# Attention with beacons and a gelu MLP on one core: first loads moved to the hardware DMA queue, and the first MLP group one pair of heads earlier

## The chip, the cores and the metric

The kernel runs on one core of a Trainium2 chip. The metric is device time in microseconds (us), and lower is better. The engines are TensorE (PE; its weight loads are shown as PEld), VectorE (DVE), ScalarE (ACT), GpSimd (POOL) and SyncE (SP). Transfers that POOL issues run on the software DMA queue, those that SP and ACT issue on the hardware queue.

## The reference

There are 8 batches, 8 heads, 576 queries, 16 beacon keys and head width 64. All inputs are float32.

```python
scale = 1.0 / np.sqrt(D)
k_all = np.concatenate([beacon_k, k], axis=2)          # 16 + 576 keys
v_all = np.concatenate([beacon_v, v], axis=2)
scores = scale * np.matmul(q, k_all.transpose(0, 1, 3, 2))
causal = np.zeros((S, Nb + S), dtype=bool)
causal[:, Nb:] = np.triu(np.ones((S, S), dtype=bool), k=1)
scores = np.where(causal, -1000000000.0, scores)
a = np.exp(scores - scores.max(-1, keepdims=True))
a /= a.sum(-1, keepdims=True) + 1e-09
attn_out = np.matmul(a, v_all)
x = attn_out.transpose(0, 2, 1, 3).reshape(B * S, H * D)   # 4608 x 512
h = x @ w_in                                               # w_in 512 x 2048
g = h * (1.0 / (1.0 + np.exp(-1.702 * h)))
out = g @ w_out                                            # w_out 2048 x 512
```

## The kernel before

**Tiles and steps.** Attention is worked in 32 steps, one for each pair of heads: pair i belongs to batch i // 4. In one step, `qk_chunk` (L289) makes the transposed scores in four chunks into the two PSUM buffers `s`; `exp_chunk` (L302, ACT) turns them into `E` in float16; `mask_chunk` cuts the causal diagonal out, on DVE (L318, a minimum with the tile `keep`) or on POOL (L325). `av_half` (L359) multiplies by V in four parts (two heads, two halves of the queries) into the PSUM ring `u`, which has four banks. The V tile `vb` carries 64 columns of ones beside each head's values, so the row sums of the exponentials come out of the same matmul; `ones` (L101) writes these columns once. `av_out` (L370) copies the four parts to an `O` buffer (three of them). Then DVE normalises: `z_turn` (L382, tile `zt`, twice), `z_recip` (L388, `rt`), `z_back` (L392, `rz`) and `norm` (L401, twice) write the result into `xT`.

The MLP takes 512 tokens as a group, nine groups in all. `mlp1` (L428) makes 16 tiles of the hidden layer, `mlp1_gelu` (L440, ACT) writes them to `g`, `mlp2` (L450) makes four output tiles of 16 matmuls each, which are copied to `osb` (L461, L463) and stored by SP (L468). Exponential and gelu need different ACT tables, so each change between them costs an `ACT_TABLE_LOAD`. Matmul results of the MLP use the same four `u` banks as AV.

**How q, k and V come in.** All inputs are cast to float16 on the way in, by the software queue that POOL issues. Batches 0 and 1 (`NB2` = 2) are loaded by `load_qk6` (L130) into a buffer `g`, six tokens to a partition row; PE transposes them (`tr_pe`, L148) and `tr_pe_out` (L156) copies them to `qT` and `kT`. Batch 0 is loaded as heads 0 to 2, 2 to 4 and 4 to 8, batch 1 at once. Their beacon keys come by `load_bk6` (L136, tile `bkn`), are transposed by PE (L165) and copied by DVE (L168). From batch 2 on, `load_qk` (L114, tiles `n0` for q and `n1` for k) loads four heads at a time; DVE transposes 32 x 32 squares (L211, `sq`), DVE or POOL puts them in order (L220, `t0`, `t1`), SP writes them to DRAM (L230, `d`) and reads them back in place (L237). The beacon keys of these batches come by `load_bk` (L120) into `bk`, which has 32 rows for each head of four, 16 of them zero, and DVE transposes them (L226). V comes by `load_v` (L176 for beacons, L179 in five pieces), the weights by `load_w1` (L186) and `load_w2` (L193) in four pieces each.

**The order.** Each engine runs its instructions in order. That order is written at build time by a planner: every piece of work is a `Work` with an engine (or a choice of engines), an assumed duration, a key (when it is due), the works it `needs` and those it comes `after`, and a buffer that it takes. `issue` (from L792) repeatedly takes the work that can start first by the planner's own clock. The list `ends` says behind which pair each MLP group comes: with `ends[0] = 6`, group 0 follows the scores of pair 5; its four output tiles are placed in the four pairs ahead of the next group, pairs 7 to 10. Group 1 follows the scores of pair 10. `FILL` matmuls on a tile of zeros (`warm`, L865) may be put where the planner sees PE idle in the first 60 us; 42 are placed. The program keeps eight semaphores for the software queue's transfers, so each transfer that POOL issues first waits until the eighth before it has landed, and whatever stands behind it on POOL waits as well.

Of the kernel before, what the change touches and what calls it, by code (L numbers as in the profile page):

```python
# [9 lines left out]
F16 = mybir.dt.float16  # L10
F32 = mybir.dt.float32
AFT = mybir.ActivationFunctionType
ALU = mybir.AluOpType
# [3 lines left out]
def kernel(  # L17
# [11 lines left out]
    nc = tc.nc  # L29
# [28 lines left out]
    VMASK = 8  # L58
# [41 lines left out]
    def ones(t):  # L100
        nc.vector.memset(t[:, :, :, D : 2 * D], 1.0)  # L101
# [16 lines left out]

    def load_bk(x):
        nc.gpsimd.dma_start(  # L120
            out=bks[x * SQ + Nb : (x + 1) * SQ, NB2:B, :, :].rearrange("n b g d -> n (b g) d"),
            in_=beacon_k[NB2:B].rearrange("b (g x) n d -> x n (b g) d", x=HG)[x],
        )
# [11 lines left out]
    def load_bk6():  # L135
        nc.gpsimd.dma_start(  # L136
            out=bkn.rearrange("n b h d -> n (b h) d"),
            in_=beacon_k[0:NB2].rearrange("b h n d -> n (b h) d"),
        )
# [21 lines left out]
    def tr_pe_beacon(b):  # L161
        u = psu.tile([P, NPAIR, Nb], F16, tag="u", name="u")
        tru[b] = u
        for p in range(NPAIR):
            nc.tensor.transpose(u[:, p, :], bkn[:, b, 2 * p : 2 * p + 2, :], ident[0:Nb, 0:Nb])  # L165

    def tr_pe_beacon_out(b):
        nc.vector.tensor_copy(out=kTs[b % 2][:, :, 0:Nb], in_=tru[b][:, :, :])  # L168
# [197 lines left out]

    def av_out(i, x, half, eng):
        if i not in Os:
            Os[i] = op_.tile([P, 2, S], F32, tag="O", name="O")
        copy[eng](  # L370
            out=Os[i][:, x, AQ[half] : AQ[half + 1]], in_=avu[(i, x, half)][:, :]
        )

# [121 lines left out]
    SPL, CAP = 2.5, 2.0  # L495

    def use(buf, *ws):
        buf.users += ws
# [6 lines left out]
    pk = {}  # L505
    mkeep = Work("POOL", 0.3, -4.95, make_keep)
    midn = Work("POOL", 0.6, -5.95, lambda: make_identity(nc, ident))

    bk6 = Work("POOL", 0.57, -5.97, load_bk6, dma=0.25)

    def first_loads(b):
        k0 = 4 * b
        kl = (-6, -4.4)[b]
        gb6 = Buf("g")
        lds = {}
        for (h0, h1) in ((0, 2), (2, 4), (4, H)) if b == 0 else ((0, H),):
            for w in (1, 0):
                x = Work(
                    "POOL", 0.7, kl + 0.1 * h0 + 0.02 * (1 - w) + (h0 == 4),
                    lambda b=b, h0=h0, h1=h1, w=w: load_qk6(b, h0, h1, w),  # L520
                    alloc=gb6 if not lds else None, dma=0.37 * (h1 - h0),
                    after=list(lds.values())[:1],
                )
                for p in range(h0 // 2, h1 // 2):
                    lds[(p, w)] = x
        ub = Buf("u")
        x = Work("PE", 0.3, k0, lambda b=b: tr_pe_beacon(b), [bk6, midn], alloc=ub)
        y = Work("DVE", 0.25, k0, lambda b=b: tr_pe_beacon_out(b), [x], alloc=kTb[b])
        use(ub, y)
        for p in range(NPAIR):  # L530
            for w in (1, 0):
                ub = Buf("u")
                kk = 4 * b + p - 0.5
                x = Work(
                    "PE", 0.55, kk, lambda b=b, p=p, w=w: tr_pe(b, p, w), [lds[(p, w)], midn],
                    alloc=ub, after=[x],
                )
                use(gb6, x)
                z = Work(
                    dict(ACT=0.66, DVE=0.76), 0, kk,  # L540
                    lambda eng, b=b, p=p, w=w: tr_pe_out(b, p, w, eng),
                    [x], alloc=qTb[b] if (w, p) == (0, 0) else None,
                    after=[y] if w == 1 else [pk[(b, 0, 0)]] if p else (),
                )
                use(ub, z)
                pk[(b, p, w)] = z
        pk[b] = y

    for b in range(B):
# [5 lines left out]
        for g in range(2) if b >= NB2 else ():  # L555
            for w in (1, 0):
# [25 lines left out]
                if w == 1:  # L582
                    if bkB is None:
                        bkB = [
                            Work("POOL", 0.55, 4.3, lambda x=x: load_bk(x), after=[ld_], dma=0.2)
                            for x in range(HG)
                        ]
                    need = [Work(
                        "DVE", 0.25, k0, lambda b=b, g=g: tr_beacon(b, g),
                        bkB, after=cp[:1],  # L590
                    )]
# [35 lines left out]
    on = [Work("DVE", 2.7, (0.2, 1.5)[x], lambda x=x: ones(vbs[x])) for x in range(2)]  # L627
# [9 lines left out]
    for i in range(NSTEP):  # L637
# [36 lines left out]
        Ob, zb = Buf("O"), [Buf("zt"), Buf("rt"), Buf("rz")]  # L674
        evs = []
        zn = []
        for x in range(2):
            for half in range(2):
                mm = av_list(x, half)
                u_ = Buf("u")  # L680
                js = sorted({j for (j, lo, hi, col) in mm})
                av = Work(
                    "PE", sum(hi - lo for (j, lo, hi, col) in mm) / 2400 + 0.05,
                    i + 1.05 + 0.2 * x + 0.1 * half,
                    lambda i=i, x=x, half=half: av_half(i, x, half),
                    [r for j in js for r in ready[j]] + vb_, alloc=u_, after=avs[-1:],
                )
                avs.append(av)
                avp.setdefault(i, []).append(av)
                use(Eb, av)  # L690
                use(vbb[b], av)
                evs.append(Work(
                    dict(DVE=0.45, ACT=0.46), 0, i + 0.5,
                    lambda eng, i=i, x=x, half=half: av_out(i, x, half, eng), [av],
                    alloc=Ob if not evs else None, after=evs[:1],
                ))
                use(u_, evs[-1])
            zn.append(Work(
                "DVE", 0.74, i + 0.48, lambda i=i, x=x: z_turn(i, x), evs[-2:],
                alloc=zb[0] if not zn else None, after=zn[:1],  # L700
            ))
        zr = Work("DVE", 0.2, i + 0.45, lambda i=i: z_recip(i), zn, alloc=zb[1])
        zk = Work("DVE", 0.75, i + 0.45, lambda i=i: z_back(i), [zr], alloc=zb[2])
        use(Ob, *zn)
        use(zb[0], zr)
        use(zb[1], zk)
        for x in range(2):
            nw = Work(
                dict(DVE=0.78), 0, i + 0.45, lambda eng, i=i, x=x: norm(i, x, eng),
                [zk], alloc=xTb[b] if p + x == 0 else None,  # L710
                after=[norms[b * NPAIR][0]] if p + x else (),
            )
            norms.setdefault(i, []).append(nw)
            use(zb[2], nw)
            use(Ob, nw)
# [3 lines left out]

    ends = [6, 11, 15, 19, 23, 27, 31, 32, 32]
# [69 lines left out]
    def issue():  # L792
        free = dict(PE=1.0, ACT=1.0, DVE=1.0, POOL=0.7, SP=0.7)
        landed = dict(POOL=[0.0] * 8, SP=[0.0] * 8)
        given = {r: [] for r in rings}
        dma_free = dict(POOL=0.0, SP=0.0)
# [3 lines left out]
        while todo:  # L800
# [43 lines left out]
            if w.dma:  # L844
                f = max(dma_free[eng], t + d + dict(SP=0.7, POOL=1.6)[eng]) + w.dma
                dma_free[eng] = f
                w.t1 = f + dict(SP=SPL, POOL=0.4 if t < 40 else 1.0)[eng]
                landed[eng].append(w.t1)
# [12 lines left out]
    nc.vector.memset(bks, 0.0)  # L861
# [38 lines left out]
```

## Time and profile before

| what | value |
|---|---|
| median of 13 runs | 378.74 us (376.81 to 379.7) |
| profiled execution | 379.7 us, span 378.0 us |
| busy PE, DVE, ACT, POOL | 359.5, 256.0, 232.4, 153.4 us |
| software queue | 18.62 MB, 47.4% of 16 engines over the span |
| hardware queue | 23.79 MB, 19.3% |
| first exponential | starts at 9.56 us |
| first matmul of MLP group 0 | 43.09 us |
| first output matmul (L450) | 63.80 us |
| MLP group 1 begins | about 94.6 us |

The span is what the profile covers; the execution's own time is 1.7 us longer. The page divides the span into 40 slices of 9.45 us; a digit is the busy share of a slice in tenths. "The chain of waits" follows the work that ended last back in time. A group such as `128x576 f16<-128x576 f16` gives the shapes of what is written and read. Times to landing are from the issue on the engine to the end of the transfer. MB of the software queue are counted in float16, as written.

### The profile page before, as it was taken

The page shows a single profiled execution, that of the slowest core. Times are in us where ns is not written, and L with a number is a line of the kernel's source. Part 1 is how long each engine was busy: PE and PEld are TensorE (multiplying, and loading weights), DVE is VectorE, ACT ScalarE, POOL GpSimd, SP SyncE. Part 2 cuts the span into 40 slices and gives each one's busy share as a digit, 9 for nine tenths or more (in the row PEclk, how much of TensorE's full clock was granted, in tenths as well). Part 3 has the DMA queues.
Part 4 walks back from the last instruction along what each step waited for, and adds up shares of the span by engine and source line. Part 5 has one row for each costly group of instructions (what it writes and reads, how often), then busy time and mean ns, then how long its engine had stood idle before and what let it go on. Part 6 is the DMA issues. An engine that isn't in the chain of part 4 may idle for free.

```text
span 378.0 us, 6003 instructions
## 1 busy us (share of the span) xinstructions
PE 359.5 (95%) x2290; PEld 177.4 (47%) x2290; DVE 256.0 (68%) x421; ACT 232.4 (61%) x345; POOL 153.4 (41%) x271
## 2 busy tenths in 40 slices
PE   7896999859999999999999999999999999999995
PEld 3443544325444444444444784444454454444442
DVE  5479896398998996899779976992698075000021
ACT  3878868425877587658765776677676743626300
POOL 9866763456256923592368235820331010000000
PEclk9967799989999999999999999999999999999999
DMA  8999799939459974596559855962010002000012
GB/s 88 165 205 167 104 208 242 219 69 138 98 161 246 139 166 141 116 128 127 180 109 134 147 155 117 128 113 62 30 56 29 0 29 83 0 29 28 27 58 83
DMA packets 68908, 42.79 MB, mean 113 GB/s; under 512 B 41744, under 2 KB 61200, under 8 KB 68880
## 3 DMA queue, kind: packets, MB, share of 16 engines
q0 software_dynamic: 50640, 18.62, 47.4%
q1 hardware_dynamic: 18240, 23.79, 19.3%
q8 instruction: 18, 0.29, 0.3%
q14 instruction: 10, 0.08, 0.1%
HBM read 44.40 MB, written 16.61 MB: 161 GB/s over the span
## 4 chain that ended last, share of the span: by engine, by line
PE 71%; DVE 12%; DMA 10%; POOL 4%; ACT 2%; issue 1%; POOLq 0%
PE u L428 29%; PE u L450 28%; PE u L359 8%; PE s L289 5%; DMA w<-in_moe_w_out_dram 4%; DMA n<-in_k_dram 3%; DVE zt L382 3%; DMA g<-in_k_dram 3%; DVE xT L401 2%; ACT E L302 2%; DVE O L370 2%; POOL vb L179 1%; DVE t L220 1%; DVE rz L392 1%; DVE sq L211 1%
## 5 line engine op out<-in xcount | busy, mean ns | idle before, releaser
L302 ACT ACTIVATE E<-s 128x1024 f16<-128x1024 f32 (+3 forms) x128 | 104.1, 864 | 48.6 <-PE s L289 47.3
L450 PE MATMUL u<-w,g 128*128 128x512 f16 x576 | 130.0, 380 | 0.2 <-DMA w<-in_moe_w_out_dram 0.2
L428 PE MATMUL u<-xT,w 128*128 128x512 f16 (+1 forms) x640 | 126.5, 358 | 0.0
L440 ACT ACTIVATE g<-u 128x512 f16<-128x512 f32 x144 | 85.3, 597 | 43.3 <-PE u L428 42.9
L325 POOL TENSOR_SCALAR_AFFINE_SELECT E<-E 128x256 f16<-128x256 f16 (+2 forms) x153 | 63.7, 435 | 87.7 <-ACT E L302 87.6
L428 PEld LDWEIGHTS <-w 128*128 128x128 f16 x640 | 61.9, 98 | 60.6 <-issue 0.9
L450 PEld LDWEIGHTS <-g 128*128 128x128 f16 x576 | 54.5, 98 | 65.8 <-issue 4.7
L463 DVE COPY osb<-u 128x512 f32<-128x512 f32 x29 | 19.8, 682 | 66.6 <-PE u L450 66.4
L359 PE MATMUL u<-E,vb 128*128 128x336 f16 (+4 forms) x448 | 57.7, 275 | 7.2 <-DVE osb L463 3.6
L370 DVE COPY O<-u 128x240 f32<-128x240 f32 (+1 forms) x88 | 36.8, 439 | 33.2 <-PE u L359 30.5
L359 PEld LDWEIGHTS <-vb 128*128 128x128 f16 (+1 forms) x448 | 38.3, 100 | 30.0 <-issue 15.1
L382 DVE STREAM_TRANSPOSE zt<-O 64x576 f32<-64x576 f32 x64 | 49.3, 770 | 3.1 <-ACT O L370 1.6
L401 DVE TENSOR_TENSOR xT<-O,rz 64x576 f16<-64x576 f32 x64 | 50.2, 785 | 0.9
L220 POOL COPY t<-sq 128x576 f16<-128x576 f16 x18 | 23.7, 1315 | 50.2 <-DVE sq L211 41.9
L289 PE MATMUL s<-qT,kT 64*128 64x80 f16 (+5 forms) x384 | 38.4, 296 | 3.2 <-ACT E L302 1.5
L211 DVE STREAM_TRANSPOSE sq<-n 128x576 f16<-128x576 f16 x48 | 34.9, 748 | 6.1 <-DMA n<-in_k_dram 5.7
L179 POOL DMA_DIRECT2D vb<-in_v_dram x40 | 35.0, 885 | 9.9 <-DMA w<-in_moe_w_out_dram 5.4
L220 DVE COPY t<-sq 128x576 f16<-128x576 f16 x30 | 28.9, 965 | 0.4
L289 PEld LDWEIGHTS <-kT 64*128 64x128 f16 x384 | 13.0, 96 | 27.3 <-issue 21.1
L392 DVE STREAM_TRANSPOSE rz<-rt 128x576 f32<-128x576 f32 x32 | 24.4, 761 | 0.5
L370 ACT COPY O<-u 128x336 f32<-128x336 f32 (+1 forms) x40 | 15.4, 423 | 8.1 <-PE u L359 8.0
L865 PE MATMUL u<-wu 128*128 128x512 f16 x42 | 13.2, 453 | 1.3 <-DVE wu L857 1.3
(38 smaller groups left out, 105.9 us busy)
## 6 DMA issues: line engine op xcount, KB each, us to landing
out_dram<-osb SPq DMA_DIRECT2D x36, 256.0 KB, 2.3
d<-t SPq DMA_DIRECT2D x12, 296.0 KB, 4.2
kT<-d SPq DMA_DIRECT2D x12, 296.0 KB, 3.3
n<-in_k_dram POOLq DMA_DIRECT2D x12, 288.0 KB, 5.1
n<-in_q_dram POOLq DMA_DIRECT2D x12, 288.0 KB, 6.0
d<-t SPq DMA_DIRECT2D x12, 288.0 KB, 3.0
qT<-d SPq DMA_DIRECT2D x12, 288.0 KB, 3.5
vb<-in_v_dram POOLq DMA_DIRECT2D x24, 128.0 KB, 5.2
```

The source lines that it names most:

```text
L179: nc.gpsimd.dma_start(out=vb[r : r + hi - lo, j, :, 0:D], in_=v[b, :, lo:hi, :].rearrange("h n d -> n h d"),)
L220: copy[eng](out=tqk[(b, g, w)][:, e, o : o + S].rearrange("p (r t) -> p r t", t=TPP), in_=sqs[(b, g, w)][:, :, e, :].rearrange("p t r -> p ...
L289: nc.tensor.matmul(sc[:, x, o : o + e - a], kT[r : r + 64, p, j * P : (j + 1) * P], qT[r : r + 64, p, a:e], start=True, stop=True,)
L302: nc.scalar.activation(out=Es[i][:, :, choff[ci] : choff[ci] + w], in_=scs[(i, ci)][:, :, 0:w], func=AFT.Exp, scale=0.125,)
L325: nc.gpsimd.affine_select(out=blk, in_=blk, compare_op=ALU.is_ge, fill=0.0, base=mc, pattern=[[0, 2], [1, w]], channel_multiplier=-1,)
L359: nc.tensor.matmul(u[:, lo:hi], vb[0:kw, j, :, :].rearrange("r h c -> r (h c)")[:, o : o + 2 * D], E[0:kw, x, col : col + hi - lo], start= ...
L370: copy[eng](out=Os[i][:, x, AQ[half] : AQ[half + 1]], in_=avu[(i, x, half)][:, :])
L382: nc.vector.transpose(zst[i][0][64 * x : 64 * x + 64, :, :], Os[i][64 * (1 - x) : 64 * (1 - x) + 64, x, :])
L401: vec[eng].tensor_tensor(out=xT[r : r + 64, p, c : c + S], in0=Os[i][r : r + 64, x, :], in1=zst[i][2][r : r + 64, :], op=ALU.mult,)
L428: nc.tensor.matmul(u[:, o : o + w], w1t[:, kp, nt * P : (nt + 1) * P], xT[:, kp, m : m + w], start=(kp == 0), stop=(kp == NKP - 1),)
L440: nc.scalar.activation(out=gts[g][:, nt, :], in_=hu[(g, nt)][:, :], func=AFT.Gelu_apprx_sigmoid)
L450: nc.tensor.matmul(o[:, :], gts[g][:, nt, mt * P : (mt + 1) * P], w2t[:, nt, :], start=(nt == 0), stop=(nt == NNT - 1),)
```

## The change

Its parts are these.

- The first pair (heads 0 and 1) of k and q of batch 0 is loaded in float32 on the hardware queue, k by SP and q by ACT, into two `O` buffers (`load_f32`), and cast to float16 by ACT (k) and DVE (q) (`cast_f32`).
- The beacon keys of batches 0 and 1 are loaded in float32 by SP into two `osb` buffers and cast, batch 0 by ACT, batch 1 by ACT or DVE (`cast_bk6`). Those of the other batches are loaded by SP into the third `O` buffer, now twice, so that all 32 rows of each head are filled, and cast as one tile (`cast_bk`); the memset of `bk` goes.
- The columns of ones are written as float32 words that hold two float16 values each.
- Batch 1's q and k are loaded as heads 0 to 4 and 4 to 8 instead of at once.
- `ends[0]` is 5: MLP group 0 follows the scores of pair 4. The other groups stay.
- The planner gets other due times and another model of the hardware queue, so that the order on all engines changes up to MLP group 1. Code for a second way of doing AV is added (`av_both` and others), but with `NBOTH = 0` nothing of it is built.

In the order that results, on POOL the first transfers are k and q of heads 2 and 3, then V, then the select that makes `keep`; the second half of batch 1's k and q stands behind the four pieces of w1, and all four loads of batch 2 stand ahead of w2. On PE all transposes of batch 1 stand ahead of MLP group 0, pairs 5 and 6 behind it. The number of matmuls is the same, warm-ups included.

```diff
-    VMASK = 8
+    ONES = 0.007826805114746094
...
-        nc.vector.memset(t[:, :, :, D : 2 * D], 1.0)
+        nc.vector.memset(t.bitcast(F32)[:, :, :, D // 2 : D], ONES)
...
+    stg = {}
     def load_bk(x):
-        nc.gpsimd.dma_start(
-            out=bks[x * SQ + Nb : (x + 1) * SQ, NB2:B, :, :].rearrange("n b g d -> n (b g) d"),
-            in_=beacon_k[NB2:B].rearrange("b (g x) n d -> x n (b g) d", x=HG)[x],
+        if x == 0:
+            stg["bk"] = op_.tile([P, 2, S], F32, tag="O", name="O")
+        n = (B - NB2) * (H // HG)
+        for y in range(2):
+            nc.sync.dma_start(
+                out=stg["bk"].rearrange("p x s -> p (x s)")[
+                    x * SQ + y * Nb : x * SQ + (y + 1) * Nb, 0 : n * D
+                ].rearrange("n (a d) -> n a d", d=D),
+                in_=beacon_k[NB2:B].rearrange("b (g x) n d -> x n (b g) d", x=HG)[x],
+            )
+    def cast_bk(eng):
+        copy[eng](
+            out=bks[:, NB2:B, :, :].rearrange("p b g d -> p (b g d)"),
+            in_=stg["bk"].rearrange("p x s -> p (x s)")[:, 0 : (B - NB2) * (H // HG) * D],
         )
...
-    def load_bk6():
-        nc.gpsimd.dma_start(
-            out=bkn.rearrange("n b h d -> n (b h) d"),
-            in_=beacon_k[0:NB2].rearrange("b h n d -> n (b h) d"),
+    def load_f32(w, eng):
+        s = op_.tile([P, 2, S], F32, tag="O", name="O")
+        stg[w] = s
+        dict(SP=nc.sync, ACT=nc.scalar)[eng].dma_start(
+            out=s.rearrange("p x s -> p (x s)")[0:TP, 0 : 2 * TR * D].rearrange(
+                "p (h c) -> p h c", h=2
+            ),
+            in_=(q, k)[w][0, 0:2].rearrange("h (p t) d -> p h (t d)", t=TR),
+        )
+    def cast_f32(w, eng):
+        if 0 not in nat6:
+            nat6[0] = gp.tile([TP, 2, H, TR * D], F16, tag="g", name="g")
+        copy[eng](
+            out=nat6[0][:, w, 0:2, :].rearrange("p h c -> p (h c)"),
+            in_=stg[w].rearrange("p x s -> p (x s)")[0:TP, 0 : 2 * TR * D],
+        )
+    def load_bk6(b):
+        s = sp.tile([P, DMODEL], F32, tag="osb", name="osb")
+        stg["b", b] = s
+        nc.sync.dma_start(
+            out=s[0:Nb, :].rearrange("n (h d) -> n h d", d=D),
+            in_=beacon_k[b].rearrange("h n d -> n h d"),
+        )
+    def cast_bk6(b, eng):
+        copy[eng](
+            out=bkn[:, b, :, :].rearrange("n h d -> n (h d)"), in_=stg["b", b][0:Nb, :]
         )
...
-    SPL, CAP = 2.5, 2.0
+    SPL, CAP = 2.0, 2.0
+    NBOTH = 0
+    HWQ = 3
...
-        for (h0, h1) in ((0, 2), (2, 4), (4, H)) if b == 0 else ((0, H),):
+        for (h0, h1) in ((2, 4), (4, H)) if b == 0 else ((0, 4), (4, H)):
...
-    on = [Work("DVE", 2.7, (0.2, 1.5)[x], lambda x=x: ones(vbs[x])) for x in range(2)]
+    on = [Work("DVE", 1.2, (-9, -7)[x], lambda x=x: ones(vbs[x])) for x in range(2)]
...
-    ends = [6, 11, 15, 19, 23, 27, 31, 32, 32]
+    trp[(0, 1, 1)].after.append(qks[(0, 1)])
+    bkB[0].after.append(exps[0][3])
+    ends = [5, 11, 15, 19, 23, 27, 31, 32, 32]
...
-    nc.vector.memset(bks, 0.0)
```

## The prediction

> **What bounds the kernel now.** I read the page's tenths first, then the busy time by stretch, then the chain of waits, then TensorE's waits and the DMA rows.
>
> ```profile
> PE   7896999859999999999999999999999999999995
> DMA  8999799939459974596559855962010002000012
> ```
>
> TensorE (PE) is full from slice 11 on, about 95 us; the DMA engines are full in most of the first eight slices, to about 75 us. The stretches say the same in us.
>
> ```profile
> 43.00:58.00 15.00, 15.00 (x80) 7.20 (x77) 14.61 (x24) 11.18 (x19) 9.93 (x13) 1.00 1.03 178
> 72.00:80.50 8.50, 3.27 (x22) 1.52 (x21) 5.78 (x11) 1.76 (x4) 2.71 (x5) 0.99 0.51 125
> 80.50:95.00 14.50, 14.47 (x91) 6.96 (x91) 12.70 (x26) 7.19 (x11) 10.28 (x18) 0.89 1.12 141
> 95.00:160.00 65.00, 64.51 (x387) 30.55 (x385) 58.01 (x95) 46.30 (x68) 32.05 (x51) 1.00 0.71 151
> 40.00:45.00 5.00, 5.00 (x42) 2.19 (x37) 4.92 (x8) 4.60 (x7) 4.81 (x10) 0.72 0.43 40
> ```
>
> The columns are the stretch, its length, busy PE, PEld, DVE, ACT and POOL, granted clock, DMA share, GB/s. After 95 us PE has 64.51 of 65.00: nothing is to be had there but by starting earlier. Before 95 us PE is busy 81.4 us, 13.2 of these with warm-up matmuls (L865) that compute nothing; so 68 us of work fill 95 us. The best single hole is 72.00:80.50, with 3.27 of 8.50; and DMA has one at 40.00:45.00, 40 GB/s.
>
> ```profile
> 47.21 15.15 DMA w<-in_moe_w_out_dram
> 62.64 11.96 DMA n<-in_k_dram
> 74.63 0.78 DVE sq L211
> 79.90 0.59 DVE osb L463
> 80.53 1.24 PE u L359 x5
> ```
>
> The chain of waits crosses the hole. The load of batch 3's k (n) is issued at 62.64, behind the four w2 loads, and lands at 74.6. VectorE (DVE) has reached that tile's transpose at 68.9 and runs in order, so everything behind it waits:
>
> ```profile
> 74.63 0.78 DVE L211 STREAM_TRANSPOSE sq<-n 128x576 f16<-128x576 f16 x1 [5.72 <-DMA n<-in_k_dram]
> PE u L359 <- DVE osb L463: 3.6, 1, 3.6
> PE u L359 <- DVE O L370: 1.6, 1, 1.6
> ```
>
> Those are the two longest of PE's waits but for a 1.8 us one on q at 18 us. The late PSUM copies (L370, L463) hold the four u banks, and PE stands.
>
> **What the change has to move: three marks.** T, the start of MLP group 0 (43.1 us before). M2, its first output matmul (63.8). M3, the start of MLP group 1 (94.6). From M3 on both programs give PE the same 1648 matmuls in the same order, 283.4 us before, so what M3 gains, the end gains, unless a later wait takes it back.
>
> **Start to T.** Removed from POOL: two issues of 0.76 and 0.65 (k, q of the first pair), bkn 0.57, four bk issues of 0.55, together 4.2 us; the keep select (0.31) moves behind the V issues. Added: SP issues eleven loads (k, two bkn, eight bk), ACT one (q). SP issues take 0.35 to 0.68 each here and SP's next work is at 46 us, which hides them (without that, 11 x 0.5). ACT's one goes ahead of its table load (1.28); both end near 2.7 us, before k can land (else 0.6 on ACT). Not shown here: a load from HBM on the hardware queue. The nearest row is the output store, 256 KB in 2.3 us; two of 288 KB together take perhaps 3, so 3.5 to 5 us. DVE drops the bk memset (0.48) and halves the words of the two memsets of ones (2.19 each, so 1.1). The new casts (96x768, 16x512, 128x768, f32 to f16) have no row; bounds 0.4 and 1.0, from the 128x512 osb copy (0.69) and 128x1024 exponential (1.02); I take 0.8. They add waits: ACT stands for k, then bkn, then, ahead of pair 1's exponentials, for the eight bk loads; DVE for q and bkn, with the copy of qT behind it. All of these should land by 10 us. k, q and bk borrow the three O buffers, which AV 0 needs only at 14. The first exponential then starts near 7.2 instead of 9.56.
>
> That is not on the path: its cover is the load of V, and were that gone, 2.3 us more could be had. The first AV waits for V of batch 0, whose last load lands at 8.8+5.7 = 14.5. Here a rule speaks against the change. The row first, the software queue in 0 to 10 us (packets, MB, share of 16 engines):
>
> ```profile
> q0 software_dynamic: 3429, 0.92, 97.3%
> ```
>
> The Trainium skill, "DMA: Bandwidth & Descriptors", section "Issuing engines are not separate DMA queues", says that loads from any engine interleave on the same 16 engines and other issuers save only sequencer time. By issue time alone V would land 2.0 earlier, at 12.5 (about 370.5 at the end). By the rule the 0.6 MB still go ahead of V: 0.3 us of earlier POOL issue and some 0.7 of engines that stood empty until 3 us are gained, 0.2 goes to bk, which now writes all 128 rows; V lands at 13.7 (371.4). I take the rule's, as engines at 97% leave no room; range 12.5 to 15.5.
>
> The software queue lets eight loads be under way; this V issue waited 2.06 us for the eighth before it, and the masks (L325) stood behind it on POOL:
>
> ```profile
> 21.37 0.89 POOL L179 DMA_DIRECT2D vb<-in_v_dram  x1 [2.06 <-DMA g<-in_k_dram]
> 22.27 1.80 POOL L325 TENSOR_SCALAR_AFFINE_SELECT E<-E 128x256 f16<-128x256 f16 x5
> ```
>
>  In the order after, half of batch 1's q and k (2 x 1.5 us) goes behind w1, so the w1 pieces, each 2.6 to 2.9 us before (29.4, 32.3, 34.5), land at about 25.1, 27.7 and 30.3. The last masks of pairs 2 and 3 come right after these, so AV of pair 3 ends near 33 (38.1 before). What DVE then has to run in order, from the copy of AV 0 (15.2) to the norms of pair 3: 20.6 us by its rows (zt 0.77, rz 0.78, xT 0.75, rt 0.27, kT and qT 0.76, O 0.4), with some 3.5 of waits: T = 39.3. Before, a like list took from 14.9 to 42.9. So T gains 3.8 (1.5 to 5.5).
>
> **T to M2.** Before, pair 5 ran ahead of the MLP; now it comes behind, and no output matmul is planned before pair 7. The cost: MLP 13.9 plus 0.7 for a clock not yet full, then last gelu and table load (1.95, as at 58.35 to 60.30), then the exponentials of two pairs (2 x 3.4), one copy between them (0.36) and the scores that wait for the last bank (0.2): 1.95+6.8+0.36+0.2 = 9.3. M2 = 39.3+14.6+9.3 = 63.2, against 63.8. PE's own work then (AV 4 and AV 5 at 1.53, scores) and 21 warm-ups lie beside this. On POOL four copies of batch 2 (1.18 each) come ahead of pair 5's masks and wait for DVE's squares, 9.5 us from T on; they end near 50, the masks are due at 57. So by M2 nearly all of T's gain is spent on one pair of exponentials that PE has nothing to hide under.
>
> **M2 to M3.** Unhindered: four output matmul groups at 3.56, three steps of scores and AV at 2.45, and 1.9 at the end: 23.5, so M3 = 86.7. Before took 94.6-63.8 = 30.8; the 7.3 more are the hole (5.9), a w2 piece that came late (4.0 for 3.56), 0.6 of slow clock (the group at 82.64 took 4.17) and 0.3 in small waits. The skill's "TensorE: Matmul & The Clock Gate" (Part 1) would give an idle PE half clock for about 3.4 us, a loss of 1.7, so 1.1 more to gain (370.3 at the end); the trace shows 0.6, and I use that.
>
> Is the hole gone? DMA is full from 3 to 74.6 us before but for some 3 us at 40 to 44.4, when POOL sat behind masks and had nothing queued; here are 36 to 52 us in 40 slices:
>
> ```profile
> DMA  9999999999664561540009799999999999989999
> ```
>
>  After, all four batch 2 loads and the first w2 are queued by 37 us, while the queue has work to 44. So that hole closes; with 0.7 from the start and 1.0 to 1.5 for the doubled bk, batch 3's k lands near 72 (69.8 to 73.5). DVE reaches its transpose after AV of pair 6 and its two zt: M2+7.7 = 70.9. PE feels it only past 71.7, since three banks are still free. So a wait of 1 us stands on DVE, about 0.3 to 0.6 of it on PE. M3 = 87.3.
>
> **Sum.** 94.6-87.3 = 7.3 us. Nothing is charged after M3: batch 3 and 4 loads follow PE's pace, and DMA has idle time at 75 to 81 and 100 to 110 to take them earlier. If that cover were gone, at most the 7.3 would be given back. The profiled execution took 379.7 (span 378.0 and 1.7 around it): 372.4. The median of the runs is 1.0 lower: 378.74-7.3 = 371.4.
>
> **Rivals.** (1) The hole stays in part. Batch 3's k takes 12 us from issue to landing as before; its issue is tied to the last exponential of pair 6 (about 63.5), so it lands at 75.5, PE loses 4: 375.5. For it: the queue is just as full. Against: w2 is then done. (2) More is gained: V lands at 12.5, T is 37.5, k at 70: M3 = 84.5, 368.7. (3) Slower: DMA is the whole pace of the first 75 us, and the added bytes on shared engines make every landing 1.5 us later instead of earlier. Place: V of batch 0, then w1. T = 44.6; pair 5 behind the MLP makes M2 = 68.5; k issued at 68.8 lands 12 later, 80.8, where PE needs it by 77: M3 = 68.5+23.5+3.9+0.6 = 96.5, or 380.6. It decides from T at about 43 together with that 12 us. Against it stand the closed hole and the half of batch 1 moved behind w1. (4) The later loads do not follow and the gain is given back: 378.5.
>
> **How the numbers follow.** The forecast has 0.51, (1) 0.20, (2) 0.10, (3) 0.15, (4) 0.04. About 0.2% (0.8 us) is what a measurement of this kernel can tell from no change. Faster 0.81, same 0.04, slower 0.15. The likeliest case is 371.4; with V, T and the landing at their bounds 369 to 374; taking in most of (1) and (2), 367.5 to 377.
>
> **What would show it.** Right: the first exponential near 7 us, V at 13 to 14, T near 39, no DMA hole in the forties, M2 near 63, L211's wait on n under 2 us, M3 near 87, and from M3 to the end 283 us as before. Wrong: T above 42, a wait over 3 us of AV on osb or O between 65 and 80, or a new PE wait after M3.

## The result, and the profile after

| | before | after |
|---|---|---|
| median of the runs of this comparison | 377.91 us (48 runs, 375.56 to 380.48) | 373.27 us (11 runs, 372.53 to 374.2) |
| profiled execution, span | 379.7, 378.0 us | 372.79, 371.1 us |
| first exponential | 9.56 | 8.33 us |
| T, start of MLP group 0 | 43.09 | 41.60 us |
| M2, first output group | 63.80 | 64.85 us |
| M3, start of MLP group 1 | 94.59 | 88.29 us |
| from M3 to the end | 283.4 | 282.8 us |

The ratio is 0.9876, 95% interval 0.9857 to 0.9895: faster by 1.2%, 4.6 us. The forecast was 371.4, with 367.5 to 377.0 as its range. In the changed kernel three matmuls of group 0 run at 39.62 already; then PE waits 1.16 us for the last norm of pair 3. T is taken at 41.60, from where the other 61 run through. Lines of `after` have other numbers: L401 is AV (L359 before), L516 and L538 the two MLP halves (L428, L450), L253 the transposes of squares (L211), L344 the exponential (L302), L367 POOL's mask (L325), L459 and L551 the copies to `O` and `osb` (L370, L463), L489 the norm (L401).

The tenths of TensorE (PE) and of DMA:

```profile
PE   7786899999999999999999999999999999999996
DMA  9999999979569943794479646931100011000012
```

PE had an 8 and a 5 at 66 to 85 us before; now every slice but the last is full from the sixth on, 46 us. The stretches, in the columns of the prediction (stretch, length, busy PE, PEld, DVE, ACT, POOL, clock, DMA share, GB/s), the first row from `before`, the others from `after`:

```profile
63.80:94.59 30.79, 25.30 (x164) 12.10 (x161) 22.86 (x42) 13.96 (x20) 16.24 (x31) 0.94 1.15 149
64.85:88.29 23.44, 23.44 (x164) 11.67 (x161) 22.78 (x42) 14.20 (x21) 18.89 (x34) 1.00 1.14 122
72.00:80.50 8.50, 8.50 (x56) 3.97 (x56) 8.33 (x16) 4.26 (x6) 7.64 (x12) 1.00 0.57 104
40.00:45.00 5.00, 3.84 (x19) 1.66 (x17) 4.96 (x8) 4.41 (x7) 4.30 (x6) 1.00 1.12 209
```

From M2 to M3 PE is never idle and its clock is full: 23.44 us for what took 30.79 before. Of the 7.35 us between them, 5.49 were idle time of PE (30.79 less 25.30); the other 1.86 are the same 164 matmuls, which took longer at a mean clock of 0.94. DMA's hole at 40 to 45 (40 GB/s before) is filled, 209 GB/s. In the chain of waits (start, duration, what), the crossing over batch 3's load is gone. The chain now comes from the last beacon load, over ACT's cast and exponential and POOL's mask, to the last w1 piece, from there over POOL and DVE to T, and then runs along PE:

```profile
6.77 4.69 DMA O<-in_beacon_k_dram
15.61 1.02 ACT E L344
16.70 0.33 POOL E L367
17.02 15.33 DMA w<-in_moe_w_in_dram
32.63 0.74 POOL vb L221
40.60 0.96 DVE xT L489
41.60 13.32 PE u L516 x61
```

The square that VectorE (DVE) stood 5.7 us for has no wait in its brackets, in the timeline of DVE (start, busy, instruction); it comes straight after the `zt` ahead of it:

```profile
71.58 1.56 DVE L470 STREAM_TRANSPOSE zt<-O 64x576 f32<-64x576 f32 x2
73.17 0.78 DVE L253 STREAM_TRANSPOSE sq<-n 128x576 f16<-128x576 f16 x1
```

The load was issued at 65.95 and landed at 70.3, 4.4 us later, where it took 12 before: the w2 pieces that it stood behind were through. PE's longest waits now all lie before T (its waits on POOL's masks and on ACT's exponentials were 0.5 and 0.9 us in all up to there before):

```profile
PE u L401 <- POOL E L367: 3.5, 4, 1.2
PE s L331 <- ACT E L344: 2.8, 6, 0.9
PE u L401 <- DMA vb<-in_v_dram: 1.3, 2, 1.0
PE u L516 <- DVE xT L489: 1.2, 1, 1.2
```

So the part behind M2 came as forecast, and the start did not: T is 41.6, not 39.3. The first 10 us show what was late. Queues (packets, MB, time of their packets as a share of 16 engines):

```profile
q0 software_dynamic: 2413, 0.55, 120.3%
q1 hardware_dynamic: 1413, 0.58, 32.5%
q10 hardware_dynamic: 208, 0.29, 11.2%
```

The software queue moved 0.55 MB in the time in which it moved 0.92 before. Counted as float32 read from HBM that is 1.10 for 1.84, and with the hardware queue's 0.87 it makes 1.97: nearly the same bytes over the same engines. V of batch 0 is on the software queue, and its loads took longer from issue to landing (the last column):

```profile
O<-in_beacon_k_dram SPq DMA_DIRECT2D x8, 48.0 KB, 6.5
vb<-in_v_dram POOLq DMA_DIRECT2D x3, 128.0 KB, 8.6
```

These V loads took 5.3 before. The last of V landed at about 15.8 (its last AV matmuls start at 15.85); before it was 14.5. And the eight beacon loads stop ACT, with pair 1's first exponential behind the cast, and POOL's w1 issues stop for V (the bracket is idle time and what ended it):

```profile
14.87 0.83 ACT L136 CAST bk<-O 128x768 f16<-128x768 f32 x1 [3.41 <-issue]
15.61 1.02 ACT L344 ACTIVATE E<-s 128x1024 f16<-128x1024 f32 x1
12.41 0.75 POOL L228 DMA_DIRECT2D w<-in_moe_w_in_dram  x1 [1.19 <-DMA vb<-in_v_dram]
15.51 0.75 POOL L228 DMA_DIRECT2D w<-in_moe_w_in_dram  x1 [0.73 <-DMA vb<-in_v_dram]
```

The profile calls ACT's wait "issue" (in the chain above, what follows the 4.69 us of the load), but the last beacon load was issued at 6.77 and the slowest took 7.9 us: 14.67.

### The profile page after: what moved, and what is told of

Read it like the earlier page. It is cut to its first block, busy times and chain, and to the rows that moved or that the text cites. A ratio compares the mean times of both kernels' runs of the same rounds, so it can differ in the third digit from the quotient of the medians.

```text
span 371.1 us, 6029 instructions
## 1 busy us (share of the span) xinstructions
PE 354.9 (96%) x2290; PEld 175.5 (47%) x2290; DVE 254.2 (68%) x422; ACT 233.3 (63%) x348; POOL 155.9 (42%) x266
## 4 chain that ended last, share of the span: by engine, by line
PE 83%; DMA 7%; DVE 5%; ACT 2%; issue 2%; POOL 0%; SPq 0%; ACTq 0%
PE u L516 34%; PE u L538 32%; PE u L401 10%; PE s L331 6%; DMA w<-in_moe_w_in_dram 4%; ACT E L344 2%; DMA O<-in_q_dram 1%; PE u L1043 1%; DVE xT L489 1%; DMA O<-in_beacon_k_dram 1%; DVE zt L470 1%; DVE O L459 1%; DVE t L262 1%; DVE rz L480 0%; DVE osb L551 0%
## 5 line engine op out<-in xcount | busy, mean ns | idle before, releaser
L344 ACT ACTIVATE E<-s 128x1024 f16<-128x1024 f32 (+3 forms) x128 | 103.5, 863 | 44.4 <-PE s L331 43.5
L538 PE MATMUL u<-w,g 128*128 128x512 f16 x576 | 129.2, 379 | 0.0
L516 PE MATMUL u<-xT,w 128*128 128x512 f16 (+1 forms) x640 | 126.2, 358 | 1.2 <-DVE xT L489 1.2
L367 POOL TENSOR_SCALAR_AFFINE_SELECT E<-E 128x256 f16<-128x256 f16 (+2 forms) x150 | 65.9, 458 | 88.8 <-ACT E L344 88.2
L516 PEld LDWEIGHTS <-w 128*128 128x128 f16 x640 | 62.1, 98 | 62.5 <-issue 2.1
L538 PEld LDWEIGHTS <-g 128*128 128x128 f16 x576 | 54.3, 98 | 64.9 <-issue 3.2
L551 DVE COPY osb<-u 128x512 f32<-128x512 f32 x30 | 20.4, 681 | 65.0 <-PE u L538 64.8
L459 DVE COPY O<-u 128x240 f32<-128x240 f32 (+1 forms) x88 | 36.4, 438 | 35.7 <-PE u L401 33.1
L401 PE MATMUL u<-E,vb 128*128 128x336 f16 (+4 forms) x448 | 55.2, 268 | 5.4 <-POOL E L367 3.5
L489 DVE TENSOR_TENSOR xT<-O,rz 64x576 f16<-64x576 f32 x64 | 50.2, 784 | 0.9
L401 PEld LDWEIGHTS <-vb 128*128 128x128 f16 (+1 forms) x448 | 37.1, 98 | 25.0 <-issue 12.2
L262 POOL COPY t<-sq 128x576 f16<-128x576 f16 x21 | 27.8, 1325 | 48.4 <-DVE sq L253 33.8
L331 PE MATMUL s<-qT,kT 64*128 64x80 f16 (+5 forms) x384 | 36.6, 283 | 3.8 <-ACT E L344 2.8
L253 DVE STREAM_TRANSPOSE sq<-n 128x576 f16<-128x576 f16 x48 | 34.8, 746 | 0.4
L262 DVE COPY t<-sq 128x576 f16<-128x576 f16 x27 | 27.5, 1017 | 0.3
L480 DVE STREAM_TRANSPOSE rz<-rt 128x576 f32<-128x576 f32 x32 | 24.3, 760 | 0.5
L459 ACT COPY O<-u 128x336 f32<-128x336 f32 (+1 forms) x40 | 15.5, 423 | 5.2 <-PE u L401 4.8
L1043 PE MATMUL u<-wu 128*128 128x512 f16 x42 | 13.3, 441 | 1.3 <-DVE wu L1036 1.3
```

The lines of the kernel that those rows point to most:

```text
L253: nc.vector.transpose(sqs[(b, g, w)][:, c * n : (c + 1) * n, :, :], nat[(b, g, w)][:, c * n : (c + 1) * n, :],)
L262: copy[eng](out=tqk[(b, g, w)][:, e, o : o + S].rearrange("p (r t) -> p r t", t=TPP), in_=sqs[(b, g, w)][:, :, e, :].rearrange("p t r -> p ...
L331: nc.tensor.matmul(sc[:, x, o : o + e - a], kT[r : r + 64, p, j * P : (j + 1) * P], qT[r : r + 64, p, a:e], start=True, stop=True,)
L344: nc.scalar.activation(out=Es[i][:, :, choff[ci] : choff[ci] + w], in_=scs[(i, ci)][:, :, 0:w], func=AFT.Exp, scale=0.125,)
L367: nc.gpsimd.affine_select(out=blk, in_=blk, compare_op=ALU.is_ge, fill=0.0, base=mc, pattern=[[0, 2], [1, w]], channel_multiplier=-1,)
L401: nc.tensor.matmul(u[:, lo:hi], vb[0:kw, j, :, :].rearrange("r h c -> r (h c)")[:, o : o + 2 * D], E[0:kw, x, col : col + hi - lo], start= ...
```

## The experiments

My theory: the gain is the hole at 72 to 80 us, where DVE stood in order before a load that had not landed; whatever keeps it from standing there gains the same. The rival: the gain is the earlier start and the earlier landings that the moved loads give. (Letters and numbers of theories in an expectation are those that it explains itself.) Of every run the profile gives T, M2 and M3; the medians are to be compared by their ratios to the kernel before, which ran beside each on the same chip.

| run | median us | ratio, 95% interval | T | M2 | M3 | M2 to M3 |
|---|---|---|---|---|---|---|
| before, again | 377.26 | 0.9988, 0.9957 to 1.0019 | 40.0 | 60.8 | 91.7 | 30.9 |
| before, squares late | 371.83 | 0.9842, 0.9816 to 0.9868 | 41.4 | 62.1 | 87.4 | 25.3 |
| before, squares late, ones as words | 370.79 | 0.9826, 0.9795 to 0.9858 | 42.3 | 64.0 | 88.9 | 24.9 |
| before, group 0 behind pair 4 | 373.67 | 0.9901, 0.987 to 0.9933 | 40.0 | 63.9 | 88.3 | 24.4 |
| before, pair 4, squares late, words | 375.70 | 0.9937, 0.9912 to 0.9961 | 40.8 | 64.7 | 89.2 | 24.5 |
| after, again | 373.00 | 0.9874, 0.982 to 0.9928 | 41.3 | 65.2 | 88.7 | 23.4 |
| after, ones as float16 | 373.30 | 0.9882, 0.9852 to 0.9912 | 41.9 | 65.2 | 88.6 | 23.4 |
| after, first pair on the software queue | 372.54 | 0.9869, 0.9841 to 0.9896 | 40.0 | 63.9 | 87.4 | 23.4 |
| after, group 0 behind pair 5 | 372.32 | 0.9855, 0.9831 to 0.9879 | 42.1 | 63.4 | 87.7 | 24.2 |
| after, both of these | 370.80 | 0.9822, 0.9791 to 0.9853 | 40.6 | 62.0 | 89.4 | 27.4 |
| after, both, squares late | 371.11 | 0.9827, 0.9794 to 0.9861 | 40.8 | 61.9 | 86.8 | 24.8 |
| after, beacon loads late | 374.41 | 0.9913, 0.989 to 0.9937 | 43.1 | 67.0 | 91.3 | 24.3 |

The marks come from one execution each. Some of these executions lie well above the median of their kernel ("squares late, ones as words" by 2.1, "after, both of these" by 2.4, "after, beacon loads late" by 1.1), and that of before which the prediction shows by 1.8. A typical execution of before, from its median less the 1.7 us outside the span and the 283.3 after M3, has M3 at 377.9 - 285.0 = 92.9; with 30.85 from M2 and 20.75 from T that is M2 at 62.05 and T at 41.3. (This takes the stretches of the two profiled executions for typical.)

**The wait alone, no load changed.** In the kernel before, batch 3's first squares are planned behind the norms of pair 7:

```diff
                 use(nb_, *tr)
+                trs[(b, g, w)] = tr
...
+    for g in range(2):
+        for w in range(2):
+            trs[(3, g, w)][0].after.append(norms[7][1])
```

> The kernel before with one change: DVE's squares of batch 3's q and k (L211) are planned behind the norms of pair 7, so DVE no longer stands in order for that load. Loads, queues and MLP order up to there as before. Theory A (the gain is the hole of TensorE at 72 to 80 us, which comes from DVE waiting for that load): most of the change's gain appears here without any of its loads, 3 to 5 us faster than before, 373 to 375, and the 3.6 and 1.6 us waits of AV for osb and O are gone. Theory B (the gain is the earlier start and the earlier landings): within 1 us of before, because the hole is only filled with another wait. Theory C (one pair fewer ahead of the MLP): also no change.

It took 371.83: 5.9 us gained, in the median more than the whole change, though the intervals overlap. DVE's wait on `n` is gone, and with it PE's 3.6 and 1.6 us on DVE's copies; of PE's waits these are the longest:

```profile
PE u L148 <- DMA g<-in_k_dram: 2.0, 2, 1.6
PE u L359 <- POOL E L325: 1.6, 2, 1.2
PE s L289 <- ACT E L302: 1.3, 4, 0.5
```

Between M2 and M3 PE waits 0.3 us in all. DMA's own hole in the forties is still there (tenths of 36 to 52 us in 40 slices):

```profile
DMA  9999999977996393005957999996999999999999
```

So an early landing was not what was needed: the same load landed at 72.3, 12.2 us after its issue, and DVE came to it at 81.83. This is what my theory said.

**Group 0 one pair earlier, no load changed** (`ends = [6, 11, ...` to `[5, 11, ...` in the kernel before).

> The kernel before with MLP group 0 behind pair 4 instead of pair 5, and no load changed. If the whole gain of the change came from the moved pair (which puts batch 3's squares later on DVE against their load), this gives the 4.6 us too: about 373. If the loads are what lets the group start early, T stays at about 43, a pair more stands behind the MLP, M2 comes 1 to 2 us later than 63.8, and the hole shrinks by only as much: about 377 to 379. I expect the second, as the w1 pieces still land at 29 to 34.5 here.

M2 came 1.9 us later than the typical 62.05, as expected. The rest was missed, and it is the most telling of the runs: 373.67, against 373.27 of the changed kernel, with intervals that overlap. With pair 5 behind the MLP, DVE has that pair's work to do after T, and comes to the square at 71.95, just after the load has landed (71.8). The only wait on `n` left in the whole execution lies at 40 us, on batch 2 (from the DVE instructions of tile `n`: waited for, us, times):

```profile
  DMA n<-in_k_dram: 0.5, 1
```

One number in `ends` gives about all that the change gave.

**The two parts undone, one by one.** First `ends[0] = 6` in the changed kernel:

> The changed kernel with MLP group 0 behind pair 5 again (ends[0] = 6), all its loads as changed. Theory A: the batch 3 load still lands before DVE needs it, so this is within 2 us of the changed kernel (372 to 375.5); theory C: the gain is lost, 377 to 379. Should DVE come to the batch 3 tile earlier than in the changed kernel, a wait of 1 to 3 us on it stands there again.

Then k and q of the first pair by POOL again (the SP and ACT loads and their casts go; `for (h0, h1) in ((0, 2), (2, 4), (4, H))`):

> The changed kernel with k and q of heads 0 and 1 back on the software queue with the cast in the transfer; beacons, ones and the order of the MLP as changed. Theory A: nearly no loss, 0 to 1.5 us slower than the changed kernel (373 to 375), since the first exponential is not on the path and the same bytes go over the same engines. Theory B: at least half of the gain is lost, over 375.5. The first exponential should start at 9 to 10 us instead of 8.3.

They took 372.32 and 372.54, with no hole in either. So the loads, with the order that they bring, also close it without the moved pair: each half of the change gives the whole gain alone, and together they give no more. Each interval overlaps with that of the changed kernel, so neither 0.95 nor 0.7 us is established by itself. In the second, the loads that are left on the two queues take less time, in the first 16 us:

```profile
O<-in_beacon_k_dram SPq DMA_DIRECT2D x8, 48.0 KB, 4.2
vb<-in_v_dram POOLq DMA_DIRECT2D x3, 128.0 KB, 6.5
```

V takes 6.5 us from issue instead of 8.6, but POOL issues it 1.6 us later, behind k and q, so that its last piece lands only 0.7 us earlier (15.1). AV 0 starts at 16.11 and is done no sooner. ACT's cast of the beacons starts at 12.54 without a wait, and T is 40.0; V does not account for that T. The loads of the first pair were themselves hardly quicker: 4.4 and 5.1 us on the hardware queue, 4.2 and 4.7 (medians of heads 0 to 4) on the software queue. The first exponential is 0.5 us later (8.86), and T is none the later for it.

**Both undone together.**

> The changed kernel with two of its parts undone together: the first pair of k and q back on the software queue, and group 0 behind pair 5 again. One by one they gave 0.7 and 0.95 us. If these two are what the change loses against the kernel before with late squares (371.8, which is 1.4 under the changed kernel), the two add up and this gives 371.6 to 372. If the loss sits elsewhere (the beacon keys on the hardware queue, with ACT waiting 3.4 us for them), the two overlap and this stays at about 372.4.

370.80, the interval 0.9791 to 0.9853 just clear of the changed kernel's 0.9857 to 0.9895: the two cost it some 2 us together. The profiled execution (373.2) shows the hole half open again:

```profile
  DMA n<-in_k_dram: 2.2, 1
  DMA n<-in_q_dram: 1.2, 1
PE u L538 <- DVE O L459: 2.9, 2, 1.5
```

The 2.2 us are those on batch 3's k, at 72.5. The 1.2 us lie at 43.9, on batch 2's q, and are no part of the hole; the expectation of the next run takes them for batch 3's.

The two sides of the wait, counted from T of each execution: when batch 3's k lands (issue plus time to landing), and when DVE comes to its square.

| run | lands at T + | DVE comes at T + |
|---|---|---|
| before; again | 31.5; 30.4 | 25.8; 26.3 |
| before, group 0 behind pair 4 | 31.8 | 31.9 |
| before, squares late | 30.9 | 40.5 |
| after; again | 28.7; 29.1 | 31.6; 32.3 |
| after, group 0 behind pair 5 | 26.2 | 28.5 |
| after, both of these | 31.8 | 29.7 |

DVE waits where its time is the smaller of the two. The moved pair alone brings DVE some 6 us later and leaves the landing where it was; the loads, with their order, bring the landing 3 to 5 us earlier and, with pair 5 ahead of group 0, DVE 2 to 3 us later. Either is enough to end the wait. With both undone the landing is back at 31.8.

**The same with late squares.**

> The changed kernel with group 0 behind pair 5, the first pair of k and q on the software queue, and batch 3's first squares planned behind the norms of pair 7. Without the last edit it took 370.8 in the median, and its profile showed DVE waiting 2.2 and 1.2 us for batch 3's k and q and two output groups delayed by 1.5 us each. If these waits are there in most executions, 2 to 3 us are gained: 368 to 369. If they were of that one execution (it took 373.2) or are made good by another order, it stays at 370.5 to 371.

The wait on batch 3's `n` is gone (0.8 us on batch 2's q stay, at 43.8), M2 to M3 is 24.8 instead of 27.4, and the profiled execution took 371.0 (span 369.3); but the median is 371.11, not 368 to 369. Either the hole stood half open in that one execution more than in most, or the other order gave its gain back; one profile does not tell. This kernel, the one above it and "before, squares late, ones as words" are within each other's intervals: three ways to about 371, each below both kernels of the comparison in the median, the one above with an interval just clear of the changed kernel's.

**The beacon loads late.** In the changed kernel the eight loads wait for an `O` buffer after pair 2's AV; they are issued at 19.7 instead of 2.2 to 6.8 (before, POOL issued four at 36.6 to 41.4).

```diff
...
+                    if i == 2 and len(evs) == 1:
+                        bkL[0].after.append(evs[0])
...
-    bkB[0].after.append(exps[0][3])
```

> The changed kernel with the eight loads of the later batches' beacon keys put into the O buffer behind that of pair 1, so that they wait until the casts of the first pair and pair 0 have freed it (about 15 to 20 us), and are cast then. In the changed kernel they go out from 2.2 us on, land as late as 14.8, compete with V of batch 0, and hold ScalarE for 3.4 us. If V is late because of them, V lands 1 us or more earlier (15 instead of 16), ScalarE's 3.4 us wait goes, MLP group 0 starts 0.5 to 2 us earlier than 41.6 and the time is 0.5 to 2 us below the changed kernel (371.5 to 373). If the engines are simply full, V lands at the same time and so does everything else: 372.5 to 374.

At the start all is as hoped:

```profile
vb<-in_v_dram POOLq DMA_DIRECT2D x3, 128.0 KB, 5.9
```

against 8.6, from the same issue times: the last of V lands at 12.9 instead of 15.8. All of AV 0 runs through from 13.23 (it started its last part at 15.85), and ACT's 3.4 us are gone. But the rest was missed: T came at 43.1 (in an execution 1.1 us above the median) and the kernel is 1.1 us slower than the changed one. The edit also gave the planner another order, with other waits of PE:

```profile
PE u L401 <- POOL E L367: 3.6, 2, 2.1
PE s L331 <- ACT kT L198: 2.0, 1, 2.0
```

So it shows that the beacon loads hold V up by some 3 us, and not what that costs at the end. The earlier V did not bring T forward here; a run with the old order and these loads moved was not made.

**The ones.** In the kernel before, with late squares; the order of every engine is the same as there:

```diff
-        nc.vector.memset(t[:, :, :, D : 2 * D], 1.0)
+        nc.vector.memset(t.bitcast(F32)[:, :, :, D // 2 : D], 0.007826805114746094)
```

> The kernel before with two edits: batch 3's first squares planned behind the norms of pair 7 (as in the earlier run at 371.8), and the columns of ones written as words. The order of every engine is that of the earlier run. The two memsets cost DVE 2.19 each before and 1.12 as words, so DVE is 2.1 us ahead in the first 10 us. If DVE's start holds the way to group 0, up to 1 us is gained: 371. If the first AV waits for V at 14.5 anyway, nothing: 371.8 (within 0.5).

And the reverse in the changed kernel:

> The changed kernel with the columns of ones written as float16 values again (2 x 2.2 us on DVE instead of 2 x 1.1), orders otherwise the same. In the kernel before the words gave 1.0 us (371.8 to 370.8). If they do so by letting DVE take the first copies earlier, this loses 0.5 to 1: 373.8 to 374.3. In the changed kernel the first exponential has room, since the first AV waits for V at 15.9; then nothing: 373.3 (within 0.4).

370.79 for 371.83 with overlapping intervals, and 373.30 for 373.27: no effect in the changed kernel, and at most a small one before.

**One pair earlier, with late squares and words.**

> The kernel before with late squares, ones as words, and group 0 behind pair 4 instead of pair 5. With pair 5 it was 370.8. In the changed kernel the pair ahead costs 0.95 us (373.3 against 372.3); if that is the price of a pair of exponentials behind the MLP, which PE has nothing to hide under, it is the same here: 371.5 to 372. If the planner's other order makes it good, 370.8 or less.

Missed: 375.7. Two edits that each gain 4 to 6 us make a kernel 5 us slower than the better one. Against that better one, the stretch from T to M2 is 2.2 us longer (23.9 for 21.75), the pair of exponentials behind the MLP, and that from M3 to the end 2.7 us (284.9 for 282.2). Late squares and a late pair now both fall to DVE around M3, where its timeline has five squares between 86 and 98 us and hardly a gap, and a copy comes late for PE:

```profile
89.24 2.76 PE L428 MATMUL u<-xT,w 128*128 128x512 f16 x12
93.42 11.38 PE L428 MATMUL u<-xT,w 128*128 128x512 f16 x52 [1.42 <-DVE O L370]
```

Group 1 takes 15.6 us instead of 13.98, which is 1.6 of the 2.7 us; the rest was not traced.

**The same kernels again.**

> The kernel before, unchanged, profiled once more. The first profiled execution took 379.7, 1.8 us above the median of the runs. Theory A1: that execution had a longer hole than most (DVE's wait for batch 3's k was 5.7 us there); a typical one has a wait of about 4 us and MLP group 1 starts at about 93 instead of 94.6. Rival A2: the hole is the same 5.5 to 6 us in every execution, and the difference of 1.8 us lies elsewhere, before group 0 or after group 1.

> The changed kernel, unchanged, profiled once more. Two profiled executions of the kernel before started group 0 at 43.1 and at 40.0 with the same program, and both needed 30.8 to 30.9 us from the first output group to MLP group 1. Theory: the start of group 0 wanders by 2 to 3 us between executions with the granted clock and the landings of the first 40 us, while the stretch from the first output group to group 1 does not; so here that stretch is 23.4 to 23.6 us again, and group 0 starts anywhere from 39.5 to 42.5. Rival: the changed kernel starts group 0 at 41.6 as steadily as its loads land (within 0.4).

The kernel before, unchanged, started group 0 at 40.03 here and at 43.09 in the prediction's profile. The stretch from M2 to M3 was 30.90 and 30.79. DVE's wait was shorter (4.2 us for 5.7), but the output group after the hole lost more to the clock (5.46 us for 4.17), and the stretch came out the same. That it agrees to 0.1 us is in part chance: PE's idle time in it was 5.5 us in the one and 4.3 in the other. So rival A2 was right about where the difference lay, before group 0, and not about an equal hole. In the earlier execution PE also waited 1.8 us at once for q (0.8 here), and its granted clock was 0.50 at 20 to 25 us (1.00 here). The changed kernel's T was 41.29 and 41.60, steadier than I had expected, and its stretch 23.44 both times.

## Why the prediction was right, and where it missed

Right: faster, inside the range, and in the stretch named, by the closed hole. The hole from M2 to M3 was to give 7.3 us less 0.6; it gave 7.4, in both executions of each kernel. T to M2 was to take 23.9 and took 23.25 and 23.95, for 20.75 before: the pair of exponentials that PE has nothing to hide under. The sum is closer than its terms: group 0 took 13.3 and 14.0 us of the 14.6 allowed, in part since three of its matmuls ran ahead of T, and what follows it 9.9 instead of 9.3. From M3 to the end was to stay at 283.4 and is 282.8 and 283.0. Rivals (1) and (4) are out, since no hole is left and nothing is given back later; (2) is out, since V landed at 15.8 and not at 12.5. Of (3), the slower one, the first half happened (landings later by 1.3 us at V), and its second did not: with w2 done, batch 3's k took 4.4 us and not 12.

Of the signs listed, the DMA hole in the forties, the wait of L211 and the time after M3 came as said, and M3 nearly; the first exponential (8.33), V, T and M2 were late. The gain was 4.6 and not 7.3. Two terms make the difference: 7.3 less 1.2 at the start, less 1.7 in the base, and 0.4 more after M3 make 4.8.

- "So T gains 3.8" failed: T was 39.3 in the forecast and 41.3 to 41.6 after; against the typical 41.3 of before it gained nothing. By the forecast's own list, DVE starts at 15.2 with the copy of AV 0, works 20.6 us and waits 3.5. It started at 16.44, worked 21.0 and waited 4.1, which makes the 2.3. Behind the late start stands the step "V lands at 13.7": V landed at 15.8, outside even the range of 12.5 to 15.5. The sum charged 0.2 us to bk. But the eight loads (393 KB read) were new in this window, since before they ran at 36 to 41 us, partly in DMA's hole. At the 1.97 MB of the first 10 us they are 2 us of transfer (an estimate), and with them moved V landed at 12.9. The w1 pieces landed 2 us late as well, the last at 32.35 for 30.3, and POOL held a mask behind the V issue that waited for it (32.63). What of T each of these costs is open. The chain to T runs through the beacons, ACT's exponential and the last w1 piece, and not through V; and the run that freed V and ACT from the beacons had, with its other order, no earlier T. M3 came at 88.29 and 88.68 instead of 87.3, 1.2 us later on average.
- The size of the base. "The median of the runs is 1.0 lower" took one profiled execution less 1.0. It was 1.8 above the median of the 48 runs, and its T was 1.8 later than the typical 41.3. So of the 6.3 us between the two profiles' M3 some 1.7 (94.6 - 92.9) are not the change's.
- A third step failed within the first term: "All of these should land by 10 us". The last beacon load landed at 14.67, and ACT stood 3.4 us with an exponential behind it.

Three readings of before were off, too. "The first AV waits for V" is not in its rows: AV 0 starts at 14.01 with no idle time ahead of it, after a mask of 13.20 to 13.71; it is the changed kernel whose AV 0 waits for V, 1.3 us. Of the w1 pieces, "each 2.6 to 2.9 us", the last took 2.2 by the times beside it. And "the hole (5.9)" and "0.6 of slow clock" split the 7.3 wrongly: PE was idle for 5.49 us in the whole stretch, and the rest is mostly slow clock.

The reason for the closed hole was only half right. I closed it by an early landing (72 by the forecast, 70.3 measured) against DVE's arrival at 70.9 (73.2 measured). The runs show that DVE's arrival decides as well, and that the moved pair alone delays it enough: it was forecast as a cost, and it is one of two sufficient causes. What the split of batch 1's loads and the other due times do by themselves was not run.

Of the two rules weighed, the first stands behind the queue rows above: "Issuing engines are not separate DMA queues", in the Trainium skill's "DMA: Bandwidth & Descriptors", by which other issuers save only the time of issue. With the beacon loads away, V was issued 1.9 us earlier than before and landed 1.6 earlier; with them beside it, it landed 1.3 later, as their bytes run on the same engines. The same page's "SWDGE vs HWDGE vs iDMA" adds that each engine takes turns between the queues which the two kinds of issuers feed; the rows agree with small loads on one queue slowing those on the other, but no run here separates size from turns.

On the clock, I took 0.6 us for the output group after the hole. But AV and the scores ahead of it ran slowly as well. From the end of PE's 3.62 us wait to that of the group, in the two executions of before:

```profile
80.53:86.81 6.28, 6.28 (x31) 2.58 (x32) 4.74 (x9) 1.89 (x2) 5.21 (x8) 0.74 0.68 102
76.36:83.93 7.57, 7.57 (x31) 2.89 (x32) 4.74 (x9) 1.89 (x2) 6.28 (x9) 0.61 0.85 102
```

Length times granted clock is 4.6 us in both, so 1.6 and 3.0 us were lost after the same wait. The rule of "TensorE: Matmul & The Clock Gate" (Part 1) makes it 1.7, an estimate from its half clock for about 3.4 us: the first row agrees, and the second does not: there the clock stayed at half for 5.9 us (0.50 up to 82.0, 1.00 from 82.25). There was no "1.1 more to gain" in this, since the 30.8 us of before hold the loss whatever its size.

## What to carry to other kernels

A long wait on an in-order engine can be taken away from either side, and reordering the instruction that waits is the cheaper edit: try it alone before moving loads. Loads moved to another queue are paid for by whatever uses the DMA engines at that time, so cost them in the window in which they land, bytes and all. Size a hole's worth from more than one execution, by the stretch and not by absolute times: here the start wandered by 3 us, the stretch by 0.1, and that with different parts. And measure two such edits together: late squares and an earlier group 0 each gained 4 to 6 us, and both at once 2.4.

## What was not expected of the hardware

- A beacon load of 48 KB, in rows of 256 bytes, took 6.5 us from issue to landing, longer than the 288 KB loads of k and q (4.4 and 5.1), which were issued earlier, at 0.81, when the DMA engines were still empty.
- The casts from float32 to float16: ACT 0.83 us for 96x768 and for 128x768, DVE 0.56 for 96x768 but 0.71 for 16x512 (0.54 with the first pair on the software queue), where ACT took 0.62.
- Writing two float16 ones as a float32 word takes 1.12 us a tile where it took 2.19, and the changed kernel's time does not show it.
